# Accumulating the spatial part first and the attention part last in the last two output tiles of a gated attention + gMLP kernel

## Chip, cores and metric

The kernel runs on one core of one Trainium2 chip. The metric is device microseconds of one execution; lower is better. Times are medians over several executions.

## The reference, cut to what matters

Two branches read the same `x` (2048 x 512) and are blended by a gate:

```python
# branch A: linear attention with a softmax feature map, then an output projection
phi_q, phi_k = ...                       # from x @ wqkv and w_phi
kv  = einsum('bhsf,bhsd->bhfd', phi_k, v)
o   = einsum('bhqf,bhfd->bhqd', phi_q, kv) / den
a   = o @ wo                             # contraction over 512
# branch B: gMLP with a spatial mix over the 2048 positions
z   = gelu(x @ w_in);  z1, z2 = z[..., :688], layernorm(z[..., 688:])
gg  = einsum('ts,bsf->btf', w_sp, z2) + b_sp[None, :, None]
b   = (z1 * gg) @ w_out                  # contraction over 688
out = g * a + (1 - g) * b                # g = sigmoid(x . gate_w)
```

The kernel scales both branches so that one accumulator (a buffer in PSUM in which successive matmuls add up) holds their sum for 128 output rows (a *tile*; there are 16). It then needs ten matmuls per tile: four for `o @ wo` (the *attention part*), five for the first or last 640 of the 688 features of `(z1 * gg) @ w_out` (the *spatial part*), and one for the remaining 48 (the *remainder*).

## The kernel before: the parts that matter

Each tile's two operands are made by VectorE, and then transposed by a DMA issued from SyncE's queue. `uT` holds the spatial operand, `oT` the attention operand.

```python
def gg_half(tt, j, gp):                  # the spatial mix: 16 matmuls, 128x344
    for st in range(NT):
        nc.tensor.matmul(gp[:, 0:HF], lhsT=wspT[:, st, tt*P:(tt+1)*P], rhs=z2all[...], ...)
    nc.vector.scalar_tensor_tensor(out=ucat[tt % NU][...], in0=gp[:, 0:HF], ...)

def attn_tile(tt):
    at = psM.tile([P, 8, P], FP32, name="at", tag="kvat", bufs=1)
    # ... [cut] 8 matmuls into at
    nc.vector.reciprocal(out=rden[:], in_=at[:, :, 64:AW])
    o = work.tile([P, D], BF16, name="o")
    nc.vector.scalar_tensor_tensor(out=o[...], in0=at[...], scalar=g_el[:, tt:tt+1], in1=rden[...], ...)
    oT = work.tile([P, NG, P], BF16, name="oT", bufs=5)
    nc.sync.dma_start_transpose(out=oT[:, :, :], in_=o[:, :])
    oTs[tt] = oT

def u_T(tt):
    uT = work.tile([P, NFT, P], BF16, name="uT", bufs=11)
    nc.sync.dma_start_transpose(out=uT[:, :, :], in_=ucat[tt % NU][:, :])
    return uT

def ba_main(acc, tt, c0=0, c1=D):
    oT, uT, i = oTs[tt], uTs[tt], tt % 2
    for g in range(NG):                  # attention part, 4 matmuls
        nc.tensor.matmul(acc, lhsT=oT[:, g, :], rhs=wo_t[:, g, c0:c1], start=(g == 0), stop=False)
    for ft in range(5):                  # spatial part, 5 matmuls
        nc.tensor.matmul(acc, lhsT=uT[:, i + ft, :], rhs=w_main[i][:, ft, c0:c1], start=False, stop=False)

def ba_tile(tt, cuts=(0, D)):            # used for tiles 14 and 15 only
    for h, (c0, c1) in enumerate(zip(cuts, cuts[1:])):
        acc = acc_tile()[:, 0:c1 - c0]
        ba_main(acc, tt, c0, c1)
        ba_rem(acc, tt, slice(0, P), c0, c1)     # remainder, 1 matmul, stop=True
        ba_store(acc, tt, c0, c1, h > 0)

for i in range(NT - 1):
    # ... [cut] queries
    gg_next(...)                         # in the last round: second half of tile 15's spatial mix, then u_T(15)
    attn_tile(i + 1)                     # in the last round: attention of tile 15
    if i > 0:
        ba_step(i - 1)                   # output tiles 0 to 13, two rounds late
ba_tile(14)
ba_tile(15, cuts=(0, 384, D))            # the last tile in two pieces of 384 and 128 columns
```

The kernel fixes the order of TensorE's and ScalarE's instructions as written. Tiles 0 to 13 are accumulated two rounds after their operands were started, tile 14 one round after. Tile 15 is the extreme: its operands are started in the last round, and only tile 13's and tile 14's output matmuls stand in between.

The softmax here doesn't subtract the row's maximum and nothing guards it: scores larger than these inputs give would overflow.

## Time and profile before

| | before |
|---|---|
| median of 3 runs | 207.75 us (207.62 to 207.82) |
| span of the profiled execution | 205.5 us |
| TensorE (PE) busy | 200.6 us, 98% |
| VectorE / ScalarE / GpSimd busy | 63% / 37% / 22% |

Here are two lines of the page of the kernel before: busy time of each engine, and the shares of the chain of waits. The chain goes back from the last instruction, at each step to whatever released it.

```profile
PE 200.6 (98%) x1522; PEld 119.9 (58%) x1540; DVE 128.6 (63%) x276; ACT 75.4 (37%) x123; POOL 45.3 (22%) x73
...
PE 96%; DMA 1%; issue 1%; DVE 0%
```

The kernel is bound by TensorE. Of what remains of the chain, 1% is a wait for a DMA. It stands in the tail, as the chain of waits in order of time shows (start us, length us, what):

```profile
196.35 0.90 PE mm L493 x5
197.25 3.07 DMA oT<-o
200.32 0.05 issue
200.37 0.82 PE mm L491 x4
201.19 0.81 PE mm L493 x5
202.00 0.16 PE mm L496
```

Line 491 is the attention part, 493 the spatial part, 496 the remainder. At 200.37 TensorE starts tile 15 with its attention part, 0.05 us after the DMA of `oT` landed. The timeline of the kernel before shows what lies around it (start us, length us, engine, line, operation, count, and in brackets the engine's idle time just before and what ended it). PE is TensorE's matmuls, PEld its weight loads (the load of a matmul's first operand), DVE is VectorE, and SPq and ACTq are DMAs issued from SyncE and ScalarE. A DMA has landed when its last completion signal has come.

```profile
195.87 1.22 SPq L485 DMA_TRANSPOSE uT<-ucat  x1
...
196.14 0.75 DVE L472 SCALAR_TENSOR_TENSOR o<-at,g_el,rden 128x512 bf16<-128x512 f32 x1
...
197.25 1.19 SPq L480 DMA_TRANSPOSE oT<-o  x1
...
197.68 1.04 PE L491 MATMUL mm<-wspT,oT 128*128 128x512 bf16 x4
...
199.63 0.38 PE L496 MATMUL mm<-wspT,uT 128*128 128x512 bf16 x1
...
200.36 0.44 PEld L491 LDWEIGHTS <-oT 128*128 128x128 bf16 x4 [0.85 <-DMA oT<-o]
200.37 0.82 PE L491 MATMUL mm<-wspT,oT 128*128 128x384 bf16 x4 [0.35 <-DMA oT<-o]
...
202.76 0.35 DVE L503 TENSOR_SCALAR ob<-mm,g_inv 128x128 bf16<-128x128 f32 x1 [5.87 <-PE mm L496]
```

Tile 14 starts at 197.68. Its last matmul starts at 199.63; at 512 columns matmuls start every 0.216 us (the *pitch*; earlier in the chain, at 191.81, five take 1.08 us), so tile 15 could have started at 199.85. It started at 200.37: 0.52 us lost. The bracket says 0.35, because a matmul's own length (0.38) is longer than the pitch. For such questions, reckon with starts.

The SPq rows are only the issue of a DMA. The Trainium skill, "Perfetto Trace Analysis" (DMA Instruction — HWDGE), says that the data movement lies outside the reported window. This trace agrees: `oT`'s row is 1.19 us long, its landing came 3.07 us after its start.

For comparing runs I use one interval, the **tail**: from the start of tile 14's first matmul to the start of VectorE's last operation, which prepares the last piece to be stored. Before: 202.76 - 197.68 = 5.08 us.

### The profile page before, as it was taken

Reading aid. Unit: us, or ns where it says so; the run is one execution under the profiler, and the core shown is the slowest. Engines: PE = TensorE matmul, PEld = TensorE weight load, DVE = VectorE, ACT = ScalarE, POOL = GpSimd, SP = SyncE. Lnnn points to the kernel's source line nnn. Section 1 sums busy time; section 2 is a strip of 40 time slices with the busy share of each in tenths; the row PEclk is TensorE's granted clock in tenths of the full one; section 3 lists DMA queues with packets and bytes.
Section 4 is the critical chain, followed back from the end, with each engine's and each line's share of the span. In section 5 each row is a group of like instructions: output and inputs, shape, how many; then the busy total and the mean of one; then the engine's idle time right before and its main releaser. Section 6 shows DMA issues by size and latency. Waiting matters only on the chain.

```text
span 205.5 us, 3940 instructions
## 1 busy us (share of the span) xinstructions
PE 200.6 (98%) x1522; PEld 119.9 (58%) x1540; DVE 128.6 (63%) x276; ACT 75.4 (37%) x123; POOL 45.3 (22%) x73
## 2 busy tenths in 40 slices
PE   8999999999999999999999999999999999999994
PEld 4666666655665555656565666555455546665632
DVE  4467484838976597979797689555365654533330
ACT  3566677795222333242424132222352116002231
POOL 5020202022423334424242422222203220200000
PEclk9999999999999999999999999999999999999999
DMA  6999599999998027841243228564645756444642
GB/s 190 262 157 191 96 144 278 192 290 217 243 268 191 3 38 219 253 87 38 53 29 63 51 48 151 111 118 77 126 116 112 80 102 171 80 89 89 104 92 77
DMA packets 90099, 27.22 MB, mean 132 GB/s; under 512 B 84224, under 2 KB 90080, under 8 KB 90080
## 3 DMA queue, kind: packets, MB, share of 16 engines
q1 hardware_dynamic: 87312, 24.55, 62.2%
q10 hardware_dynamic: 2736, 2.42, 3.7%
q8 instruction: 12, 0.20, 0.4%
q14 instruction: 7, 0.06, 0.1%
q0 software_dynamic: 32, 0.00, 0.0%
HBM read 4.15 MB, written 2.10 MB: 30 GB/s over the span
## 4 chain that ended last, share of the span: by engine, by line
PE 96%; DMA 1%; issue 1%; DVE 0%
PE mm L454 36%; PE zp L191 18%; PE mm L359 13%; PE mm L493 8%; PE mm L399 7%; PE mm L491 6%; PE at L467 2%; PE kvacc L415 2%; PE zp L222 2%; DMA oT<-o 1%; PE mm L496 1%; PE zp L311 0%; PE zp L230 0%; PE pq L284 0%; PE pq L311 0%
## 5 line engine op out<-in xcount | busy, mean ns | idle before, releaser
L454 PE MATMUL mm<-z2all,wspT 128*128 128x344 bf16 x512 | 79.9, 309 | 0.0
L454 PEld LDWEIGHTS <-wspT 128*128 128x128 bf16 x512 | 49.0, 98 | 25.7 <-issue 0.4
L191 PE MATMUL zp<-w_z,xT 128*128 128x344 bf16 x252 | 38.0, 309 | 0.0
L363 ACT ACTIVATE eq<-mm 128x512 bf16<-128x512 f32 x32 | 17.4, 594 | 51.3 <-POOL eq L376 21.5
L367 DVE TENSOR_REDUCE zs<-eq 128x64 f32<-128x1024 bf16 x16 | 19.5, 1220 | 20.3 <-ACT eq L363 20.3
L191 PEld LDWEIGHTS <-xT 128*128 128x128 bf16 x252 | 24.2, 98 | 12.0 <-DVE xT L290 0.3
L459 DVE SCALAR_TENSOR_TENSOR ucat<-mm,bT,z1all 128x344 bf16<-128x344 f32 x32 | 17.4, 544 | 21.9 <-PE mm L454 21.9
L376 POOL TENSOR_TENSOR eq<-eq,ratio 128x512 bf16<-128x512 bf16 x16 | 16.9, 1055 | 49.9 <-DVE ratio L375 41.8
L363 ACT ACTIVATE ek<-mm 128x512 bf16<-128x512 f32 x32 | 17.3, 601 | 27.1 <-PE mm L359 27.1
L507 ACT ACTIVATE ob<-mm,g_inv 128x512 bf16<-128x512 f32 (+1 forms) x16 | 10.9, 680 | 33.3 <-PE mm L496 28.8
L367 DVE TENSOR_REDUCE zs<-ek 128x64 f32<-128x1024 bf16 x16 | 19.3, 1208 | 2.8 <-ACT ek L363 2.8
L493 PE MATMUL mm<-wspT,uT 128*128 128x512 bf16 (+2 forms) x85 | 20.1, 366 | 0.0
L359 PEld LDWEIGHTS <-xT 128*128 128x128 bf16 x128 | 12.2, 98 | 12.9 <-PE mm L496 0.8
L376 POOL TENSOR_TENSOR ek<-ek,ratio 128x512 bf16<-128x512 bf16 x16 | 16.9, 1056 | 2.1 <-DVE ratio L375 1.5
L359 PE MATMUL mm<-wq_p,xT 128*128 128x512 bf16 x55 | 16.0, 379 | 0.5
L399 PE MATMUL mm<-wv_sb,xT 128*128 128x512 bf16 x64 | 16.4, 379 | 0.0
L491 PE MATMUL mm<-wspT,oT 128*128 128x512 bf16 (+2 forms) x62 | 15.6, 365 | 0.7 <-DMA oT<-o 0.4
L359 PE MATMUL mm<-wk_p,xT 128*128 128x512 bf16 x61 | 16.1, 379 | 0.2
L209 DVE BATCH_NORM_STATS2 bn<-z2all 128x6 f32<-128x344 bf16 x32 | 14.9, 502 | 0.0
L206 ACT ACTIVATE z2all<-zp 128x688 bf16<-128x688 f32 x16 | 11.8, 743 | 7.2 <-PE zp L191 7.1
L264 ACT ACTIVATE z1all<-zp 128x688 bf16<-128x688 f32 x16 | 11.9, 743 | 5.1 <-PE zp L191 4.7
L493 PEld LDWEIGHTS <-uT 128*128 128x128 bf16 x85 | 8.1, 98 | 9.2
(74 smaller groups left out, 142.5 us busy)
## 6 DMA issues: line engine op xcount, KB each, us to landing
out_dram<-ob ACTq DMA_DIRECT2D x15, 128.0 KB, 1.7
wspT<-in_B_w_out_dram SPq DMA_DIRECT2D x2, 640.0 KB, 4.6
w_z<-in_B_w_in_dram SPq DMA_DIRECT2D x2, 344.0 KB, 4.2
wv_sb<-in_A_wqkv_dram SPq DMA_DIRECT2D x2, 256.0 KB, 3.6
wspT<-in_A_wo_dram SPq DMA_DIRECT2D x2, 256.0 KB, 3.8
w_z<-in_B_w_in_dram SPq DMA_DIRECT2D x2, 172.0 KB, 3.8
xs<-in_A_x_dram SPq DMA_DIRECT2D x2, 128.0 KB, 2.5
uT<-ucat SPq DMA_TRANSPOSE x16, 2.8
```

The costliest lines, as they stand in the source:

```text
L191: nc.tensor.matmul(zp[:, j, 0:n], lhsT=xT[:, dt, tt * P:(tt + 1) * P], rhs=wt[:, dt, j * HF:j * HF + n], start=(dt == first), stop=(dt == ...
L209: nc.vector.bn_stats(out=bn6[:, tt, j, :], in_=z2v[:, j, :])
L264: nc.scalar.activation(out=z1all[:, tt, :].rearrange("p (j n) -> p j n", j=2), in_=zp[:, :, 0:HF], func=AF.Gelu_apprx_tanh,)
L359: nc.tensor.matmul(ps[:, :], lhsT=xT[:, dt, tt * P:(tt + 1) * P], rhs=w[:, dt, :], start=(dt == 0), stop=(dt == NDT - 1))
L363: nc.scalar.activation(out=e[:, :, a, :], in_=ps[:, :].rearrange("p (h f) -> p h f", f=DH), func=AF.Exp, scale=1.0 - 2.0 * a)
L367: nc.vector.tensor_reduce(out=z[:].rearrange("p h a -> p (h a)"), in_=e[:].rearrange("p h a f -> p (h a) f"), axis=AX.X, op=ALU.add,)
L376: nc.gpsimd.tensor_tensor(out=e[:, :, 1, :], in0=e[:, :, 1, :], in1=ratio[:, :, None].to_broadcast([P, H, DH]), op=ALU.mult)
L399: nc.tensor.matmul(v_ps[:, :], lhsT=xT[:, dt, tt * P:(tt + 1) * P], rhs=wv_sb[:, dt, :], start=(dt == 0), stop=(dt == NDT - 1))
L454: nc.tensor.matmul(gp[:, 0:HF], lhsT=wspT[:, st, tt * P:(tt + 1) * P], rhs=z2all[:, st, j * HF:(j + 1) * HF], start=(st == 0), stop=(st == ...
L459: nc.vector.scalar_tensor_tensor(out=ucat[tt % NU][:, c0 + j * HF:c0 + (j + 1) * HF], in0=gp[:, 0:HF], scalar=bT[:, tt:tt + 1], in1=z1all[ ...
L491: nc.tensor.matmul(acc, lhsT=oT[:, g, :], rhs=wo_t[:, g, c0:c1], start=(g == 0), stop=False)
L493: nc.tensor.matmul(acc, lhsT=uT[:, i + ft, :], rhs=w_main[i][:, ft, c0:c1], start=False, stop=False)
```

## The change

Its intent: let the operand that arrives first be used first. In tiles 14 and 15 the spatial part and the remainder now start the accumulation, and the attention part ends it. All other tiles keep their order. Cut to its core:

```diff
     def ba_tile(tt, cuts=(0, D)):
         for h, (c0, c1) in enumerate(zip(cuts, cuts[1:])):
             acc = acc_tile()[:, 0:c1 - c0]
-            ba_main(acc, tt, c0, c1)
-            ba_rem(acc, tt, slice(0, P), c0, c1)
+            ba_spat(acc, tt, True, c0, c1)
+            ba_rem(acc, tt, slice(0, P), False, c0, c1)
+            ba_attn(acc, tt, False, True, c0, c1)
             ba_store(acc, tt, c0, c1, h > 0)
```

`ba_main` is split into `ba_attn` and `ba_spat`, with the start and stop flags as arguments; `ba_step` (tiles 0 to 13) calls them in the old order [cut]. The Trainium skill, "PSUM — Partial Sum Buffer" (The four PSUM rules), says that the first matmul of a group overwrites and the later ones accumulate, so the start flag has to move to the spatial part along with the order. All runs here with this order gave correct results.

More of the change, by code (lines that the diff above doesn't have):

```diff
@@ L486, in u_T, with ba_attn, ba_spat, ba_rem @@
         return uT
-    def ba_main(acc, tt, c0=0, c1=D):
-        oT, uT, i = oTs[tt], uTs[tt], tt % 2
+    def ba_attn(acc, tt, start, stop, c0=0, c1=D):
         for g in range(NG):
-            nc.tensor.matmul(acc, lhsT=oT[:, g, :], rhs=wo_t[:, g, c0:c1], start=(g == 0), stop=False)
+            nc.tensor.matmul(acc, lhsT=oTs[tt][:, g, :], rhs=wo_t[:, g, c0:c1],
+                             start=start and g == 0, stop=stop and g == NG - 1)
+    def ba_spat(acc, tt, start, c0=0, c1=D):
+        i = tt % 2
         for ft in range(5):
-            nc.tensor.matmul(acc, lhsT=uT[:, i + ft, :], rhs=w_main[i][:, ft, c0:c1], start=False, stop=False)
-    def ba_rem(acc, tt, rows, c0=0, c1=D):
+            nc.tensor.matmul(acc, lhsT=uTs[tt][:, i + ft, :], rhs=w_main[i][:, ft, c0:c1],
+                             start=start and ft == 0, stop=False)
+    def ba_rem(acc, tt, rows, stop, c0=0, c1=D):
         nc.tensor.matmul(
-            acc, lhsT=uTs[tt][rows, 5 * (1 - tt % 2), :], rhs=w_rem[rows, c0:c1], start=False, stop=True)
+            acc, lhsT=uTs[tt][rows, 5 * (1 - tt % 2), :], rhs=w_rem[rows, c0:c1], start=False, stop=stop)
     def ba_store(acc, tt, c0, c1, on_dve):
@@ L523, in ba_step @@
         accs[tt] = acc_tile()
-        ba_main(accs[tt][:, :], tt)
+        ba_attn(accs[tt][:, :], tt, True, False)
+        ba_spat(accs[tt][:, :], tt, False)
         if tt == group[-1]:
             for t in group:
-                ba_rem(accs[t][:, :], t, halves[t % 2])
+                ba_rem(accs[t][:, :], t, halves[t % 2], True)
             for t in group:
```

## The prediction

> **What bounds the kernel now.** TensorE. The page gives PE 98% busy in a span of 205.5 us, and the chain of waits is PE for 96%, DMA for 1%; the granted clock is 0.9 or more in all slices. The change touches only the tail, so I read that in order of time.
>
> Tile 14 starts at 197.68 us: four attention matmuls, five spatial ones and a remainder, with no wait for a DMA; the remainder starts at 199.63. Tile 15 comes next, and its attention operand oT is late. Its transposing DMA was issued at 197.25, once VectorE had written o (reciprocal 0.35 us and scale 0.75 us, after the attention matmuls at 195.06), and landed 3.07 us later, at 200.32. The chain has this piece: DMA oT 3.07 us, "issue" 0.05 us, then PE at 200.37. The waits view gives 0.8 us for the weight load and 0.4 us for the matmul. The pitch at 512 columns is 0.216 us (five in 1.08 us), so without the wait tile 15 could have started at 199.63 + 0.22 = 199.85. Lost: 200.37 - 199.85 = 0.52 us. Its spatial operand uT, issued at 195.87 with 2.8 us to landing, had been there since 198.67.
>
> **What the change does.** It adds and removes no instruction: the instruction order shows equal counts on all engines, with VectorE, ScalarE, GpSimd and the DMA queue unchanged, and on PE only the last 60 rows permuted. Tiles 14 and 15 run spatial, remainder, attention. The wait for tile 15's oT moves from its first weight load to its seventh; uT's becomes the first.
>
> The Trainium skill, "TensorE: Matmul & The Clock Gate" (Step-by-step), says that matmuls stay in program order and only weight loads are pulled ahead. The trace agrees: nothing of tile 15 ran in that 0.52 us, although uT had landed. So the written order decides.
>
> **Costing.** Tile 14 starts at 197.68 as before (its uT was issued at 186.17; its oT, issued at 192.42 with 4.1 us to landing, was there by 196.5). Tile 15 starts at 199.85. Six matmuls at 384 columns take 6 x 0.162 = 0.97 us (five take 0.81 in the chain), to 200.82; oT landed at 200.32. The wait is covered with 0.5 us to spare, some 0.3 us for the weight load that goes ahead. All 0.52 us lies on the critical path; what follows (the rest of tile 15, VectorE's 0.35 us, the last store of some 2 us) only shifts earlier. PSUM banks are free in time.
>
> **Predicted:** 207.75 - 0.5 = 207.25 us, range 206.85 to 207.65. Chances: faster by over 2% 0.5%, within 2% 99%, slower by over 2% 0.5%. The gain is 0.25%, hardly more than the spread of the runs (207.62 to 207.82).
>
> **What would show it.** Right: PE's idle at the start of tile 15 is gone; no wait on oT there; the DMA piece leaves the chain of waits, which becomes PE through tiles 14 and 15; the last PE matmul of the chain starts near 202.15 instead of 202.67; all before 197 us is the same. Wrong: a wait on oT at tile 15's seventh weight load, or on uT at its first; a slower pitch; a longer last store.
>
> **What would make it wrong.** oT's landing varies (2.4 to 4.1 us in this tail). At 2.4 us before, almost nothing was lost in ordinary runs and the gain vanishes; at 4.1 us up to 0.97 us is covered and the gain nearly doubles. Stores of tiles 12 and 13 share the DMA engines with this transpose. The rest is variation between runs and chips, by an estimate from the spread 0.1 to 0.2%.

## The result, and the profile after

| | before | after |
|---|---|---|
| median | 207.90 us (6 runs, 207.62 to 208.42) | 207.36 us (6 runs, 206.92 to 207.71) |
| ratio, with 95% interval | | 0.9971 (0.9954 to 0.9988) |
| span of the profiled execution | 205.5 us | 205.2 us |
| tail | 5.08 us | 4.55 us |
| TensorE busy | 200.6 us | 200.5 us |

A ratio is the mean time of one kernel's fast runs over that of the other's of the same rounds, so it is not quite the ratio of the medians. The change is a small gain: about 0.6 us by the ratio, 0.54 us by the medians.

The chain of waits of the kernel after, in order of time (line 496 is now the spatial part, 500 the remainder, 490 the attention part):

```profile
197.94 1.19 PE mm L496 x5
199.12 0.22 PE mm L500
199.34 0.86 PE mm L490 x4
200.20 0.81 PE mm L496 x5
201.01 0.16 PE mm L500
201.18 0.65 PE mm L490 x4
```

The DMA piece is gone; the chain runs through tiles 14 and 15 on TensorE alone. The timeline of the kernel after, same columns as before:

```profile
197.44 1.19 SPq L480 DMA_TRANSPOSE oT<-o  x1
...
197.87 1.25 PE L496 MATMUL mm<-wspT,uT 128*128 128x512 bf16 x5
...
200.04 0.98 PE L496 MATMUL mm<-wspT,uT 128*128 128x384 bf16 x5
...
200.85 0.33 PE L500 MATMUL mm<-wspT,uT 128*128 128x384 bf16 x1
200.85 0.58 PEld L490 LDWEIGHTS <-oT 128*128 128x128 bf16 x4
...
201.01 0.81 PE L490 MATMUL mm<-wspT,oT 128*128 128x384 bf16 x4
...
202.42 0.35 DVE L507 TENSOR_SCALAR ob<-mm,g_inv 128x128 bf16<-128x128 f32 x1 [5.34 <-PE mm L490]
```

No TensorE row of tile 15 has a bracket now. `oT` was issued at 197.44 and again took 3.1 us, so it was there at about 200.5, and its first weight load came at 200.85: covered with about 0.3 us to spare. The tail is 202.42 - 197.87 = 4.55 us, 0.53 us less.

Why do the spans differ by 0.3 only? Because the profiled execution of the kernel after was already late in the first stage, which the change doesn't touch. One piece of the chain of waits of each kernel, the same 48 matmuls, first before, then after:

```profile
36.75 7.11 PE zp L191 x48
```

```profile
36.93 7.11 PE zp L191 x48
```

It stands 0.18 us later, and tile 14 starts 0.19 us later (197.87 against 197.68). Over the 14 profiles this start lies between 36.75 and 37.81 us: 1.06 us of scatter made before the change's part of the kernel begins, twice the gain in question. From this mark to tile 14's first matmul it is 160.93 us before, 160.94 us after, and 160.92 or 160.93 us in each of the twelve experiments, so nothing is lost or won between them. The tail is free of the scatter.

### The profile page after: what moved, and what is told of

It reads as the page before. It is cut to its first block, busy times and chain, and to the rows that moved or that the text cites. A ratio compares the mean times of both kernels' runs of the same rounds, so it can differ in the third digit from the quotient of the medians.

```text
span 205.2 us, 3940 instructions
## 1 busy us (share of the span) xinstructions
PE 200.5 (98%) x1522; PEld 119.9 (58%) x1540; DVE 128.5 (63%) x276; ACT 75.6 (37%) x123; POOL 45.3 (22%) x73
## 4 chain that ended last, share of the span: by engine, by line
PE 95%; DMA 2%; issue 1%; ACTq 0%; DVE 0%
PE mm L454 36%; PE zp L191 18%; PE mm L359 13%; PE mm L496 8%; PE mm L399 7%; PE mm L490 7%; PE at L467 2%; PE kvacc L415 2%; DMA w_z<-in_B_w_in_dram 2%; PE mm L500 1%; PE zp L311 0%; PE pq L311 0%; PE zp L230 0%; ACTq L117 0%; ACTq L120 0%
```

## The experiments

Theory A says that the whole gain is TensorE's wait for tile 15's `oT`, which now passes behind six matmuls. Rival B says that the order itself helps (matmuls or weight loads that follow closer, in both tiles), without regard to a wait. All runs were timed in five rounds against the kernel before. Results were correct except for the two runs that say otherwise.

| run | median us | ratio (95%) | tail us | tile 15's `oT`, us to landing |
|---|---|---|---|---|
| only15 | 207.50 | 0.9972 (0.9954 to 0.9990) | 4.55 | 3.1 |
| only14 | 207.73 | 0.9996 (0.9980 to 1.0012) | 5.09 | 3.07 |
| first_cut | 207.48 | 0.9976 (0.9962 to 0.9990) | 4.56 | 3.1 |
| all_steps | 207.43 | 0.9972 (0.9956 to 0.9988) | 4.55 | 3.1 |
| attn_early | 207.46 | 0.9977 (0.9961 to 0.9993) | 4.56 | 2.5 |
| stale_oT (wrong result) | 207.46 | 0.9977 (0.9963 to 0.9992) | 4.55 | 3.1 |
| after_again | 207.24 | 0.9964 (0.9951 to 0.9978) | 4.56 | 3.1 |
| after_attn_early | 207.66 | 0.9983 (0.9970 to 0.9996) | 4.56 | 3.1 |
| before_late | 208.83 | 1.0041 (1.0025 to 1.0057) | 5.84 | 2.54 |
| after_late | 207.61 | 0.9985 (0.9966 to 1.0004) | 4.82 | 2.50 |
| no_uT15 (wrong result) | 208.00 | 1.0001 (0.9987 to 1.0014) | 4.99 | 3.26 |
| late_stores | 208.29 | 1.0007 (0.9984 to 1.0029) | 5.35 | 3.33 |

The intervals of the ratios are 0.3 to 0.5 us to each side, so they tell gain from no gain, but not one cure from another. The tail does that.

### One tile alone: only15, only14, first_cut

Each takes the kernel after and restores the old order where the condition is false:

```diff
-            ba_spat(acc, tt, True, c0, c1)
-            ba_rem(acc, tt, slice(0, P), False, c0, c1)
-            ba_attn(acc, tt, False, True, c0, c1)
+            if tt == 15:        # only14: tt == 14; first_cut: tt == 15 and h == 0
+                ...             # spatial, remainder, attention
+            else:
+                ...             # attention, spatial, remainder
```

> Tile 14 in the old order, tile 15 in the new. Theory A (the whole gain is tile 15's wait for its oT): as the changed kernel, ratio 0.9971 within noise of 0.0015; in the tail, from the start of tile 14's first matmul to VectorE's last store preparation 4.56 us as after (before: 5.08), no wait for oT. Rival B (the order itself makes matmuls run closer, in both tiles): half the gain, 4.8 us.

> Tile 14 in the new order, tile 15 in the old. Theory A: no gain, ratio 1.000, tail 5.08 us give or take the landing of tile 15's oT, and PE waits some 0.35 us for it with the weight load waiting 0.8. Rival B: half the gain, 4.8 us.

> Only the first 384 columns of tile 15 in the new order; tile 14 and the last 128 columns in the old. Theory A: these six matmuls in front cover the wait, so all of the gain: tail 4.56 us, ratio 0.997 within 0.0015. If the reordering elsewhere contributed: above 4.6 us.

Tile 15 alone has all of the gain (tail 4.55 us), tile 14 alone none (5.09 us). Within tile 15, the first 384 columns alone have all of it (4.56 us). The timeline of only14 has the old wait, unchanged:

```profile
197.97 1.25 PE L496 MATMUL mm<-wspT,uT 128*128 128x512 bf16 x5
...
200.66 0.82 PE L490 MATMUL mm<-wspT,oT 128*128 128x384 bf16 x4 [0.36 <-DMA oT<-o]
```

So the gain needs the six matmuls that stand at the place of the wait, and no other reordering. This speaks against rival B, which expected half in each tile.

### The order in all tiles: all_steps

On top of the kernel after, tiles 0 to 13 take the spatial part first too (their remainder stays last, for it is shared within groups of tiles):

```diff
-        ba_attn(accs[tt][:, :], tt, True, False)
-        ba_spat(accs[tt][:, :], tt, False)
+        ba_spat(accs[tt][:, :], tt, True)
+        ba_attn(accs[tt][:, :], tt, False, False)
```

> The new order in tiles 14 and 15 as changed, and in all other tiles too the spatial matmuls before the attention ones (the remainder stays last there). Theory A: those tiles' operands landed long before, no wait to cover: nothing more than the changed kernel, tail 4.56 us, ratio 0.997. If the order itself helped, another 14 tiles would show it by several tenths of a per cent.

Ratio 0.9972, tail 4.55 us: the same as the kernel after. The stretch that holds these fourteen tiles, from the first stage's mark (37.09 us here) to tile 14's start (198.02 us), is 160.93 us as in the kernel before. Fourteen more reordered tiles bring nothing, and cost nothing.

### The wait taken away without reordering: attn_early, stale_oT

attn_early takes the kernel before and starts tile 15's attention one group of matmuls earlier:

```diff
+            if i == NT - 2:
+                attn_tile(i + 1)
             gg_next(bank_tile(g_bank if i + nq < NT or i % 2 == 0 else q_bank))
-            attn_tile(i + 1)
+            if i < NT - 2:
+                attn_tile(i + 1)
```

> The old order in both last tiles, but tile 15's attention matmuls are issued one group earlier, ahead of the last 16 spatial-mix matmuls, so its oT lands some 2.3 us earlier. Theory A: the wait is gone without any reordering of the accumulation, tail 4.56 us, ratio about 0.997 (0.9955 to 0.9985). Rival B: no gain, 1.000, tail 5.08.

stale_oT lets the kernel before read tile 14's `oT` in tile 15. It computes a wrong result. (The edit did take effect: in its trace tile 15's attention part starts at 200.64, before tile 15's own `oT` landed at 201.13.)

```diff
-        oT, uT, i = oTs[tt], uTs[tt], tt % 2
+        oT, uT, i = oTs[min(tt, NT - 2)], uTs[tt], tt % 2
```

> Wrong result on purpose: the old order, but tile 15 reads tile 14's oT, landed long before, in place of its own. Nothing else changes. Theory A: tail 4.56 us, ratio about 0.997. Rival B: 5.08 and 1.000. A rival C, that the wait was a bank or a queue beside oT, also leaves 5.08.

Both keep the old order of accumulation in full, and both have the gain: tails of 4.56 and 4.55 us, ratios of 0.9977. The timeline of attn_early, with `oT` issued 3.3 us before tile 14 starts:

```profile
195.11 1.24 SPq L480 DMA_TRANSPOSE oT<-o  x1
...
198.38 1.04 PE L491 MATMUL mm<-wspT,oT 128*128 128x512 bf16 x4
...
200.34 0.38 PE L496 MATMUL mm<-wspT,uT 128*128 128x512 bf16 x1
200.34 0.64 PEld L491 LDWEIGHTS <-oT 128*128 128x128 bf16 x4
...
200.55 0.81 PE L491 MATMUL mm<-wspT,oT 128*128 128x384 bf16 x4
```

`oT` landed 0.79 us before tile 14's start, where it had landed 2.64 us after it: 3.4 us earlier, not the expected 2.3, which makes no difference once the wait is gone. Tile 15's first matmul follows tile 14's last after 0.21 us, which is the pitch. With the wait gone the old order is as fast as the new one. Rival B falls, and so does the thought that something beside `oT` held tile 15 back: stale_oT changed nothing but which buffer is read.

### Both cures at once, and a control: after_attn_early, after_again

after_attn_early is the edit of attn_early made to the kernel after; after_again is the kernel after, unchanged.

> Both cures at once: the new order and the earlier attention matmuls. Theory A: both remove the same wait, so no more than one: tail 4.56 us, ratio 0.997. If the two gains are of different kinds, they add: about 0.9945, tail 4.1. It is also the candidate for a kernel that beats both, if uT or oT is marginal anywhere.

> The changed kernel again, as a control for its neighbours in this batch: ratio 0.9975 within 0.0015, tail (tile 14's first matmul to VectorE's last store preparation) 4.56 us.

The tail is 4.56 us in both: the gains don't add, as they should not if both remove the same wait. The time of after_attn_early (0.9983) is no better than the control's (0.9964). None of its five runs was faster than the control's slowest (207.47 us). In the two profiled executions, 207.66 and 207.07 us, the difference stands before the change's part begins: the mark of the first stage is at 37.68 and 37.10 us. Why it is later, and whether that holds for the other runs, is not shown. No experiment gave a version better than the kernel after.

### Making `oT` later: before_late, after_late

VectorE writes tile 15's `o` three times instead of once, in the old order and in the new:

```diff
-        nc.vector.scalar_tensor_tensor(out=o[...], ...)
+        for _ in range(3 if tt == NT - 1 else 1):
+            nc.vector.scalar_tensor_tensor(out=o[...], ...)
```

> The old order; VectorE writes tile 15's o three times instead of once, so that its oT is issued about 1.5 us later (two times 0.75). Theory A: all of it is waited for: about +1.5 us, ratio 1.0072, tail 6.6 us, PE idle at tile 15's start about 1.9 us. Rival B gives the same here.

> The same delay of 1.5 us in the new order. Theory A: the six spatial and remainder matmuls of tile 15's first part (0.97 us) cover 0.97 us of the wait, of which 0.52 were used: against the changed kernel +1.0 to +1.1 us, against before about +0.5 (ratio 1.0024), tail about 5.6 us, with a PE idle of about 1 us at tile 15's seventh weight load; about 1.0 us less than the old order with the same delay. Rival B: the distance to the old order stays 0.5 us.

The absolute figures missed: tails of 5.84 and 4.82 us where 6.6 and 5.6 were expected. The timelines show why, first before_late, then after_late:

```profile
196.64 2.33 DVE L473 SCALAR_TENSOR_TENSOR o<-at,g_el,rden 128x512 bf16<-128x512 f32 x3
...
198.18 1.04 PE L492 MATMUL mm<-wspT,oT 128*128 128x512 bf16 x4
...
199.04 1.22 SPq L481 DMA_TRANSPOSE oT<-o  x1
...
201.62 0.82 PE L492 MATMUL mm<-wspT,oT 128*128 128x384 bf16 x4 [1.11 <-DMA oT<-o]
```

```profile
201.42 0.44 PEld L491 LDWEIGHTS <-oT 128*128 128x128 bf16 x4 [0.48 <-DMA oT<-o]
201.42 0.82 PE L491 MATMUL mm<-wspT,oT 128*128 128x384 bf16 x4
```

VectorE was 1.58 us longer (2.33 against 0.75), but `oT` was issued only 1.29 us later (0.86 us after tile 14's start, against 0.43 us ahead of it), and it landed after 2.54 us instead of 3.07. That leaves 1.29 - 0.53 = 0.76 us of real delay, and the old order paid exactly that: 5.84 - 5.08 = 0.76 us. The new order paid 0.27 us. So the two orders now lie 1.02 us apart where they had been 0.53 apart; by the ratios it is 0.56% of 208 us, or 1.2 us, with some 0.5 us of noise to each side. (0.04 us of the 1.02 is the landing, 2.54 against 2.50 us.) This is the number that separates the theories: 1.0 for theory A (the six matmuls of 0.97 us cover what they can), 0.5 for rival B.

### Why `oT` is late: no_uT15, late_stores

The shortfall of the delay raised a new question. The prediction had said that `oT` was issued once VectorE had written `o`. But `o` was finished at 196.14 + 0.75 = 196.89, and the issue came at 197.25. no_uT15 takes the kernel before and leaves out tile 15's `uT` transpose, reading tile 13's (a wrong result):

```diff
         if j == 1:
-            uTs[tt] = u_T(tt)
+            uTs[tt] = u_T(tt) if tt < NT - 1 else uTs[tt - 2]
```

> Wrong result on purpose: the old order, tile 15 reads tile 13's uT and its own uT transpose is not issued. It asks why tile 15's oT is late. Theory Q (it stands behind uT in the queue of SyncE: VectorE had written o at 196.89, uT's issue held the queue until 197.09, and oT then shares its flight with uT): oT is issued within 0.1 us of o's end, 0.7 us before tile 14 starts instead of 0.43, lands after 2.5 us instead of 3.07, and the wait is gone in the old order: tail 4.56 us, ratio 0.997. Rival P (the issue waits for a matmul of tile 13, as the chain of waits draws it): issue still 0.43 us before tile 14, landing 3.1 us, wait unchanged, tail 5.08.

The timeline of no_uT15:

```profile
197.13 0.75 DVE L472 SCALAR_TENSOR_TENSOR o<-at,g_el,rden 128x512 bf16<-128x512 f32 x1
...
197.96 1.19 SPq L480 DMA_TRANSPOSE oT<-o  x1
...
198.35 0.39 PE L496 MATMUL mm<-wspT,uT 64*128 64x512 bf16 x2
...
198.67 1.04 PE L491 MATMUL mm<-wspT,oT 128*128 128x512 bf16 x4
...
201.27 0.82 PE L491 MATMUL mm<-wspT,oT 128*128 128x384 bf16 x4 [0.26 <-DMA oT<-o]
```

Half of theory Q holds. The issue now comes 0.08 us after `o` is finished, and 0.71 us ahead of tile 14 instead of 0.43. So in the kernel before the issue of `uT` stood in the way: it held SyncE's queue from 195.87 to 197.09. The chain of waits draws the issue of `oT` as released by a matmul of tile 13; that was an inference. In no_uT15 it draws the third of five such matmuls where it had drawn the fifth: the issue moved relative to them (rival P falls). The other half fails: the flight took 3.26 us instead of 2.5, so `oT` landed hardly earlier, and the tail shrank by 0.09 us only.

What lengthens the flight? late_stores takes the kernel before and issues the stores of tiles 12 and 13 after that of tile 14:

```diff
-            nc.scalar.dma_start(out=dst, in_=ob[:, :])
+            if tt in (12, 13):
+                deferred.append((dst, ob))
+            else:
+                nc.scalar.dma_start(out=dst, in_=ob[:, :])
+            if tt == 14:
+                for d_, o_ in deferred:
+                    nc.scalar.dma_start(out=d_, in_=o_[:, :])
```

> The old order; the output stores of tiles 12 and 13 are issued only after that of tile 14, so that no store travels while tile 15's oT does. It asks why that oT took 3.07 us (3.26 without uT ahead of it) where others took 2.5. Theory S (its last packets stand behind the store of tile 12 on the DMA engines): it lands after 2.5 to 2.7 us, PE's wait shrinks from 0.5 to at most 0.15 us in the old order, tail 4.56 to 4.7 us. Rival: the store has no part, 3.1 us to landing and tail 5.08. The time itself is of less use, as the stores now stand before the last one: ratio 0.997 to 1.000.

Theory S falls. From the timeline and the chain of waits of late_stores:

```profile
198.30 1.19 SPq L480 DMA_TRANSPOSE oT<-o  x1
...
201.68 0.82 PE L491 MATMUL mm<-wspT,oT 128*128 128x384 bf16 x4 [0.62 <-DMA oT<-o]
201.82 0.34 ACTq L511 DMA_DIRECT2D out_dram<-ob  x1
```

```profile
198.30 3.33 DMA oT<-o
```

The first store after tile 14's start is tile 14's own, issued at 201.82, after `oT` had landed at 201.63; those of tiles 12 and 13 follow it. The flight was 3.33 us, not shorter. Neither the store nor the transpose ahead explains why this DMA takes 3.1 to 3.3 us here and 2.5 us in attn_early or before_late.

The kept traces show what goes with it, though no run tested it. They record 16 completion signals for each transpose. In the kernel before, 15 of the 16 for tile 15's `oT` had come 2.50 us after its issue; the last came at 3.07. A packet of 8 KB from a queue that the profile calls "instruction" (q14) starts 1.83 us after that issue and takes 0.31 us, and the last two packets of the transpose start as it ends, at 199.39. All ten traces with 3.07 to 3.34 us look so: 15 signals by 2.53 us, one late, and such a packet 1.8 to 2.2 us after the issue. The three with 2.5 us (attn_early, before_late, after_late) have no such packet while the transpose's own packets run. (The profile's view of the DMA queues lists it between 198.6 and 200.3 us of the kernel before, and lists none between 200.2 and 201.58 us of before_late.) In after_attn_early, with 3.1 us, the issue itself took 1.88 us instead of 1.24. This is an association and not a shown cause, and not the only one: the `oT` transposes of tiles 5 and 9 took 3.3 and 3.4 us in the kernel before without such a packet. By an estimate from these numbers, with the 15 signals alone `oT` would have landed at 199.75, ahead of the 199.85 at which tile 15 could start, and almost nothing would have been lost. All this bears on how large the wait was, not on whether the wait was the cause.

## Why the prediction was right

The time, 207.36 us, lies 0.11 us from the predicted 207.25 and within the range. So close a hit in absolute time is partly luck: the median of the kernel before itself went from 207.75 us (3 runs) to 207.90 (6 runs), and the interval of the ratio is about 0.35 us to each side. What was tested sharply is the gain within the trace. Point by point:

- **The size of the wait: right.** 0.52 us, worked out from starts and pitch in the trace before; the tail shrank by 0.53 us.
- **All of it on the critical path, nothing given back: right.** TensorE runs from tile 14 to the end without a wait, and VectorE's last operation moved by the whole amount.
- **Which part does it: right, and shown.** Only tile 15, only its first 384 columns (only15, only14, first_cut). Reordering tile 14 is idle.
- **It is the wait and not the order: shown.** The old order with the wait removed has the same tail (attn_early, stale_oT), both cures don't add (after_attn_early), and more reordering gives nothing (all_steps).
- **The cover of up to 0.97 us: right in size.** With 0.76 us more delay the distance of the two orders grew to 1.02 us (before_late, after_late).
- **"once VectorE had written o": wrong, without harm.** The issue came 0.36 us after that, behind `uT` in SyncE's queue (no_uT15). I read the landing time from the trace and not from this reason, so the sum didn't suffer. It did mislead me in the delay experiments, where I expected 1.5 us and got 0.76: 0.29 us of what was missing is this slack behind `uT`, the other 0.53 us is the shorter flight (2.54 instead of 3.07 us), which I had not foreseen.
- **"oT's landing varies": too cautious.** It varies from tile to tile (2.4 to 4.1 us in the tail), but for tile 15 with its neighbours unchanged it was 3.1 us in the kernel before, the kernel after, only15, only14, stale_oT, first_cut, all_steps and after_again alike.
- **"all before 197 us is the same": badly posed.** The first stage scatters by 1.06 us over the profiles, so absolute times tell nothing at half a microsecond. The same goes for the last matmul "near 202.15". The interval from tile 14's first matmul does.

## What to carry to other kernels

When a sum has contributions whose operands arrive at different times, put the one that arrives last at the end of the accumulation. Here it cost nothing, in fourteen tiles without a late operand (all_steps), but it paid only at the place where the trace shows TensorE waiting: one tile of sixteen, 0.25% of the time. The Trainium skill, "DMA: Bandwidth & Descriptors" (Rules for kernel authors), advises issuing a DMA early and waiting on its semaphore late; both halves worked here and are worth the same 0.5 us (attn_early is the first, the change the second), but not twice. For effects below the scatter of the runs, measure an interval inside the trace that starts after the scatter is made.

## What the Trainium skill lacked or had wrong

- "DMA: Bandwidth & Descriptors": for an on-chip DMA transpose of this size on trn2 I found no issue time there (its table for "previous generations" has one of 8,192 tiles). For tile 15 in the kernel before, issuing a transpose of 128x512 took 1.19 us of SyncE's queue and of 128x768 1.22 us (the former took 1.19 to 1.24 us in thirteen of the 14 profiles, 1.88 us in after_attn_early), so the next transpose in program order stood behind it for 0.28 us (issued 0.36 us after its operand was finished, against 0.08 us with the queue free in no_uT15).
- "DMA: Bandwidth & Descriptors": I found no figure for how far the landing of one and the same 128x512 transpose varies with its place in the kernel: 2.4 to 4.1 us in the tail of one trace. It was 3.26 us without the transpose ahead and 3.33 us without stores beside it, so neither is the reason. In the ten slow flights of tile 15 one of 16 completion signals was late, 3.07 us against 2.50 for the others in the kernel before, with a packet of the instruction queue in the flight; that this packet is the cause was not tested.
- "TensorE: Matmul & The Clock Gate" (Step-by-step): agrees with the runs. Matmuls kept to program order, 0.52 us of waiting with the other operand there, and only a weight load went ahead of its matmul (200.85 against 201.01 us after).
